# One softmax reciprocal per unit for all units, two kinds of eviction on either engine, and a new order table, in a one-core attention and feed-forward kernel

## The chip, the cores and the metric

The kernel runs on one core of a Trainium2 chip. The metric is the device time of one execution in microseconds, as the median of several runs. The kernel before takes 643.45 us (three runs, 642.06 to 644.78).

## What is computed

Attention with a position bias, then a feed-forward layer with a sigmoid gate. B = 4, H = 8, S = 576, D = 64; the feed-forward layer takes 2304 rows of 512 to 2048 and back.

```python
scores = scale * np.matmul(q, k.transpose(0, 1, 3, 2))
x = (psi_rel / psi_i)[..., None]              # log1p of |i - j| over log1p of i
h = np.maximum(x @ w1 + b1, 0.0)              # 32 hidden units per pair (i, j)
scores = scores + (h @ w2).transpose(2, 0, 1)[None]
attn = softmax(scores)                        # over the keys
x = np.matmul(attn, v)  ->  (2304, 512)
h = x @ w_in                                  # 512 x 2048
g = h * (1.0 / (1.0 + np.exp(-1.702 * h)))
out = g @ w_out                               # 2048 x 512
```

## The kernel before, in words

All of it is one program on five engines. A product of two float32 matrices is made as three products of float16 parts (high x high, high x low, low x high), so nearly every operand is split into a high part (one engine scales and rounds it) and a low part (VectorE subtracts, `lo_part`, L738).

**Bias.** For each of 5 chunks of 128 query rows (`c`, the last of 64), 8 (or 4) pieces `s` make 16 rows each: four `relu` (L619, on ScalarE L625 or VectorE L627), matrix products into PSUM (`products`, L636), an eviction from PSUM that scales each row (`bias_evict`, L646, always ScalarE), and a store to DRAM. The loads of the bias for a pair of heads come back later from there (`bias_load`, L718).

**Attention.** 72 units, each one batch entry, one chunk of rows and two heads. A unit is: `scores` (L946, TensorE), `reduce` for each head (L962, VectorE: adds the bias and finds the row maximum), `expo` for each head (L972, ScalarE: exponential and row sum), `inverse` (L979, VectorE: adds 1e-9 and scales, L982, then the reciprocal, L984, of the row sums in the tile `sm`), the split of the normalised rows (`exp_hi`, L989, on ScalarE L996 or VectorE L992, then `exp_lo`), a transpose by DMA (`turn`), and for two units together the product with v (`av`, L1049) and the split of its result into the tile `xT` (`x_pair`, L1086). The first 8 units are transposed on TensorE instead (`turn_pe`, `turn_out`, `turn_tail`). For units below `ONE_INV` = 16, `inverse` runs once, on both heads' sums (128x2), after both exponentials; from unit 16 on it runs twice, on 128x1, each after its own head's exponential.

**Feed-forward.** Ten blocks of rows (256, blocks 4 and 9 of 128). For each block 16 slices `f` of the hidden layer: `m1` (L1257, the first product, L1269), `tanh` (L1275, ScalarE), `gate_mul` (L1280, VectorE, L1283: it also frees the PSUM tile `hp`, of which there are two), `gate_hi` (L1287, ScalarE or VectorE), `gate_lo` (L1295, L1298: a subtraction on VectorE or GpSimd), `m2` (L1302, the second product, L1307). At the end of a block the result is evicted (`out_evict`, L1312, always ScalarE) and stored. `m1` of a block needs the whole of its `xT`, so the first matmul of block 0 waits for unit 7 and that of block 1 for unit 15.

**The weights** come as 64-bit numbers and are put together by three VectorE operations each (`merge`) and split (`w_split`).

**What sets the order.** All of this is put down as tasks with an engine, a cost and dependences (`Plan.add`, L34). `Plan.order` (L58) runs the tasks through a model of the engines and picks, whenever an engine is free, the ready task of the lowest priority number. The priorities are the 2,300 or so numbers of `TURNS` (L231), in the order in which tasks were added. `WHERE` (L220) says for the tasks that may run on either of two engines which one takes each (`either`, L553). What comes out is one fixed sequence of instructions per engine, each engine working through its own in that sequence and waiting at each instruction for what that one needs.

## Time and profile before

| what | value |
|---|---|
| runs | 642.06, 643.45, 644.78 us |
| the profiled execution's own time | 642.35 us |
| its span in the profile | 640.5 us |
| TensorE busy | 598.4 us, 93% of the span |
| VectorE busy | 516.2 us, 81% |
| ScalarE busy | 385.1 us, 60% |
| GpSimd busy | 82.2 us, 13% |
| DMA, mean rate over the span | 178 GB/s |
| first feed-forward matmul (L1269) | 114.2 us after the start |

The span is one execution on the chip. PE is TensorE, PEld its weight loads, DVE is VectorE, ACT is ScalarE, POOL is GpSimd, SP is the engine that issues most DMAs. 1.85 us of the profiled execution's own time lie outside the span. A row's "idle before, releaser" says how long the engine stood still just before the instruction and what ended that.

### The profile page before, as it was taken

The numbers are of one execution on the slowest core, as the hardware profiler recorded it, in microseconds if no ns is written. First come the engines' busy times: TensorE is split into PE (matmuls) and PEld (weight loads), VectorE is DVE, ScalarE is ACT, GpSimd is POOL, SyncE is SP. The second block draws the span as 40 slices with busy tenths as digits, with TensorE's granted clock in tenths as the row PEclk, the third lists the DMA queues.
The fourth block names the chain that finished last, engine by engine and source line by source line (L and its number), as shares of the span: only waits on it lengthen the run. The fifth ranks groups of instructions, "written<-read, shape, count | busy, mean of one in ns | idle before, by whom it ended". The sixth has DMA issues, their size and how long they took to land.

```text
span 640.5 us, 22783 instructions
## 1 busy us (share of the span) xinstructions
PE 598.4 (93%) x9648; PEld 423.2 (66%) x9648; DVE 516.2 (81%) x1381; ACT 385.1 (60%) x851; POOL 82.2 (13%) x123
## 2 busy tenths in 40 slices
PE   5769778899999999999999989999999999999997
PEld 2225556666756676668676677768667777787775
DVE  7999988999999957885978999887987978823333
ACT  7987785789798638653745764554554656322122
POOL 3000000113211012201020111100112100111021
PEclk9769989999999999999999999999999999999999
DMA  9996966699999795999999999997996995620000
GB/s 267 306 309 175 302 188 177 109 255 243 255 254 195 140 230 145 195 197 206 212 176 257 204 229 158 202 176 136 172 223 143 174 154 105 114 44 31 2 35 18
DMA packets 239030, 113.96 MB, mean 178 GB/s; under 512 B 218576, under 2 KB 223312, under 8 KB 238928
## 3 DMA queue, kind: packets, MB, share of 16 engines
q1 hardware_dynamic: 236240, 107.83, 78.2%
q10 hardware_dynamic: 2688, 4.68, 2.1%
q8 instruction: 75, 1.23, 0.8%
q14 instruction: 27, 0.22, 0.1%
HBM read 52.85 MB, written 15.34 MB: 106 GB/s over the span
## 4 chain that ended last, share of the span: by engine, by line
PE 70%; DVE 17%; ACT 6%; DMA 4%; issue 2%; ACTq 0%; SPq 0%; DVEq 0%
PE op L1307 25%; PE hp L1269 24%; PE hp L1062 7%; PE sp L957 7%; DVE wide L966 3%; DVE wide L739 3%; PE sp L644 3%; ACT wide L625 2%; DMA wide<-scr 2%; PE op L644 2%; PE op L1016 1%; DVE th L1283 1%; DVE v L739 1%; DVE narrow L1199 1%; DVE narrow L1203 1%
## 5 line engine op out<-in xcount | busy, mean ns | idle before, releaser
L1269 PE MATMUL hp<-xT,w 128*64 128x256 f16 (+1 forms) x3840 | 207.3, 262 | 7.6 <-DVE th L1283 4.3
L1269 PEld LDWEIGHTS <-w 128*64 128x64 f16 x3840 | 189.7, 110 | 26.7 <-issue 16.9
L1307 PE MATMUL op<-w,gT 128*64 128x512 f16 x1728 | 203.5, 380 | 0.0
L1298 POOL TENSOR_TENSOR gT<-th,gT 128x256 f16<-128x256 f32 (+1 forms) x102 | 77.1, 757 | 551.0 <-ACT gT L1291 278.5
L1307 PEld LDWEIGHTS <-gT 128*64 128x64 f16 x1728 | 96.9, 110 | 73.9 <-issue 6.3
L975 ACT ACTIVATE wide<-wide,sm 128x576 f32<-128x576 f32 x144 | 110.7, 769 | 50.0 <-DVE sm L966 47.4
L1277 ACT ACTIVATE th<-hp 128x256 f32<-128x256 f32 (+1 forms) x160 | 57.1, 357 | 115.7 <-PE hp L1269 94.1
L1283 DVE SCALAR_TENSOR_TENSOR th<-th,hp 128x256 f32<-128x256 f32 (+1 forms) x160 | 62.1, 390 | 64.4 <-ACT th L1277 63.6
L966 DVE CUSTOM_DVE_ANT_0 wide<-sp,wide 128x576 f32<-128x576 f32 x144 | 105.7, 750 | 6.1 <-PE sp L957 4.2
L739 DVE SCALAR_TENSOR_TENSOR wide<-wide,sm,wide 128x576 f16<-128x576 f32 x128 | 106.2, 843 | 3.0 <-ACT wide L996 2.7
L957 PE MATMUL sp<-wide,narrow 64*128 64x512 f16 (+2 forms) x720 | 67.3, 326 | 6.0 <-DVE sm L966 4.0
L625 ACT ACTIVATE wide<-tab,bp 128x576 f32<-128x576 f32 x86 | 62.8, 774 | 0.0
L1062 PEld LDWEIGHTS <-v 128*64 128x64 f16 x2160 | 58.4, 111 | 5.7 <-issue 2.7
L1062 PE MATMUL hp<-wide,v 128*64 128x128 f16 (+1 forms) x2160 | 60.0, 214 | 1.7 <-DVE th L1283 1.7
L957 PEld LDWEIGHTS <-narrow 64*128 64x128 f16 (+1 forms) x960 | 28.4, 98 | 41.2 <-issue 23.5
L996 ACT ACTIVATE wide<-wide,sm 128x576 f16<-128x576 f32 x65 | 48.8, 768 | 7.8 <-DVE sm L984 5.3
L1291 ACT CAST gT<-th 128x256 f16<-128x256 f32 (+1 forms) x76 | 29.1, 383 | 27.2 <-PE op L1307 13.6
L644 PE MATMUL op<-wide,pk 128*32 128x512 f32 (+1 forms) x224 | 25.0, 522 | 11.2 <-ACT narrow L647 6.0
L992 DVE TENSOR_SCALAR wide<-wide,sm 128x576 f16<-128x576 f32 x63 | 34.5, 556 | 0.2
L1298 DVE TENSOR_TENSOR gT<-th,gT 128x256 f16<-128x256 f32 (+1 forms) x58 | 23.1, 397 | 8.7 <-ACT gT L1291 7.6
L982 DVE TENSOR_SCALAR sm<-sm 128x1 f32<-128x1 f32 (+1 forms) x128 | 19.8, 154 | 12.7 <-ACT wide L975 12.3
L627 DVE TENSOR_SCALAR wide<-tab,bp 128x576 f32<-128x576 f32 x58 | 29.1, 530 | 0.8 <-PE sp L644 0.8
(74 smaller groups left out, 496.4 us busy)
## 6 DMA issues: line engine op xcount, KB each, us to landing
wide<-scr SPq DMA_DIRECT2D x32, 576.0 KB, 5.1
scr<-narrow SPq DMA_DIRECT2D x31, 288.0 KB, 3.0
wide<-in_moe_w_out_dram SPq DMA_DIRECT2D x16, 512.0 KB, 5.8
wide<-in_moe_w_in_dram SPq DMA_DIRECT2D x16, 512.0 KB, 5.2
wide<-in_k_dram SPq DMA_DIRECT2D x16, 256.0 KB, 5.1
narrow<-in_q_dram SPq DMA_DIRECT2D x16, 256.0 KB, 4.3
out_dram<-narrow ACTq DMA_DIRECT2D x16, 256.0 KB, 3.9
wide<-scr SPq DMA_DIRECT2D x8, 288.0 KB, 4.6
```

The costliest lines, as they stand in the source:

```text
L625: nc.scalar.activation(out=h, in_=tv, func=ACTF.Relu, bias=bp[:, pb:pb + 1])
L644: nc.tensor.matmul(to[32 * r:32 * r + 32], lhsT=w2b, rhs=rhs, start=True, stop=True)
L739: nc.vector.scalar_tensor_tensor(out=out, in0=in0, scalar=scale, in1=in1, op0=ALU.mult, op1=ALU.subtract)
L957: nc.tensor.matmul(pair[64 * e:64 * e + m, a, cs], lhsT=qt[r, x, hp + e, q0:q0 + m], rhs=k_of(b, hp + e, y, cs)[r], start=i == 0, stop=i == 2,
L966: nc.vector.tensor_tensor_reduce(out=slot(("a32", u))[:, cs], in0=slot(("sp", u)).rearrange("p (h a) n -> p h (a n)", h=2)[:, a, 0:S], in1 ...
L975: nc.scalar.activation(out=t, in_=t, func=ACTF.Exp, scale=-1.0, bias=sm[:, a:a + 1], accum_out=sm[:, 2 + a:3 + a])
L1062: nc.tensor.matmul(o[64 * a:64 * a + 64, po], lhsT=vt[:, x, vc:vc + 64], rhs=t[:, 9 * y + k0, po], start=kb < 0 and i == 0, stop=kb == 3 a ...
L1269: nc.tensor.matmul(p[y0:y0 + FF, :n], lhsT=wi16[:, f // 4, cc, z, w0:w0 + FF], rhs=r, start=i == 0, stop=i == 11, skip_group_check=FF < 128,)
L1277: nc.scalar.activation(out=slot(("th", j, f))[:, :n], in_=slot(("hp", j, f))[:, :n], func=ACTF.Tanh, scale=0.851 / (XS * WIS))
L1283: nc.vector.scalar_tensor_tensor(out=th, in0=th, scalar=1.0, in1=slot(("hp", j, f))[:, :n], op0=ALU.add, op1=ALU.mult)
L1298: (nc.vector if on("low", NF * j + f) == "V" else nc.gpsimd).tensor_tensor(out=gt[:, 1, :n], in0=th, in1=gt[:, 0, :n], op=ALU.subtract)
L1307: nc.tensor.matmul(o[y0:y0 + FF, i], lhsT=gt[:, z, 128 * i + y0:128 * i + y0 + FF], rhs=wo16[:, NF - 1 - f, y, :], start=f == 0 and n3 == ...
```

## The change

Three things change in the code, and the two tables with them. `ONE_INV` goes from 16 to 72, so `inverse` runs once for both heads in all units. `bias_evict` and `out_evict` may run on either engine, by two new strings in `WHERE`. All the other strings of `WHERE` and the whole of `TURNS` are replaced. The diff also adds branches that no unit takes here (`POOL_EXP`, `RELU_POOL` and `WARM` are empty).

```diff
     WHERE = {
-        'khi': 'AAAAAAVV',
+        'evict': 'AAAAAAAAAAAAAAAAAAAAAAAAAAAVAAAAVAAV',
+        'out': 'AAAAAAAAVAAAAVVAVAVA',
+        'khi': 'AAAAAAAA',
...
     TURNS = [
-        -105731, 7219, -6608, 12047, -1336, 20364, -21356, -1727, 7198, -17301, -23943, -24621, -26077, -10464,
...
+        -5778, -1874, -6302, -696, -6131, 3502, 428, 4509, -1771, 3505, -12098, -21823, -18034, -12144, -8006, -4740,
...
-    ONE_INV, TAB_LATE = 16, False
+    ONE_INV, TAB_LATE = 72, False
...
+    EVICT = {"A": act(S, True, 1), "V": dve(S, ptr=1)}
...
     def bias_evict(c, s):
-        nc.scalar.activation(
-            out=slot(("os", c, s))[:, 0:S], in_=bias_out(c, s)[:, 0:S], func=ACTF.Copy,
-            scale=ips[:, 8 * c + s:8 * c + s + 1],
-        )
+        t, o, x = slot(("os", c, s))[:, 0:S], bias_out(c, s)[:, 0:S], ips[:, 8 * c + s:8 * c + s + 1]
+        if on("evict", 8 * c + s) == "A":
+            nc.scalar.activation(out=t, in_=o, func=ACTF.Copy, scale=x)
+        else:
+            nc.vector.tensor_scalar(out=t, in0=o, scalar1=x, scalar2=None, op0=ALU.mult)
...
-            ev = add("ACT", act(S, True, 1), lambda c=c, s=s: bias_evict(c, s), [b],
+            ev = either("evict", 8 * c + s, lambda c=c, s=s: bias_evict(c, s), EVICT, [b],
...
     def out_evict(j, i):
-        nc.scalar.activation(out=slot(("ob", j, i))[:, 0:DM], in_=slot(("op", j))[:, i], func=ACTF.Copy,
-                             scale=1.0 / (2.0 * XS * WIS * WOS))
+        t, o, x = slot(("ob", j, i))[:, 0:DM], slot(("op", j))[:, i], 1.0 / (2.0 * XS * WIS * WOS)
+        if on("out", 2 * j + i) == "A":
+            nc.scalar.activation(out=t, in_=o, func=ACTF.Copy, scale=x)
+        else:
+            nc.vector.tensor_scalar(out=t, in0=o, scalar1=x, scalar2=None, op0=ALU.mult)
...
-            ev = add("ACT", act(512, True), lambda j=j, i=i: out_evict(j, i), [pm2],
+            ev = either("out", 2 * j + i, lambda j=j, i=i: out_evict(j, i), {"A": act(512, True), "V": dve(512)}, [pm2],
```

What the new tables do to the number of instructions on an engine (in the whole program):

| kind (line before) | VectorE before | now | the others |
|---|---|---|---|
| `inverse` on 128x1 (L982 and L984 together) | 224 | 0 | |
| `inverse` on 128x2 (both) | 32 | 144 | |
| `relu` (L627) | 58 | 51 | ScalarE +7 |
| `exp_hi` (L992) | 63 | 59 | ScalarE +4 |
| `x_pair`, high part (L1095) | 12 | 9 | ScalarE +3 |
| `k_split`, high part (L832) | 2 | 0 | ScalarE +2 |
| `gate_lo`, 256 columns (L1298) | 46 | 59 | GpSimd -13 |
| `gate_lo`, 128 columns (L1298) | 12 | 16 | GpSimd -4 |
| `bias_evict` and `out_evict` | 0 and 0 | 3 and 5 | ScalarE -3 and -5 |

TensorE has the same matmuls as before, and SP the same 278 DMAs. The order on TensorE stays nearly as it was up to the first feed-forward matmul; after that, neighbours change places.

The first place where instructions stand differently is VectorE in unit 31, one of the units from 16 on. `wide` is the unit's tile of exponentials, `sm` its row sums, `th`, `hp` and `gT` are tiles of the feed-forward layer. Before:

```order
L966 ISA wide_91,sm_78<-sp,wide_90 128x576
L966 ISA sm_78 128x1
...
L982 TENSOR_SCALAR sm_78<-sm_78 128x1
L984 RECIPROCAL sm_78<-sm_78 128x1
...
L1283 SCALAR_TENSOR_TENSOR th_121<-th_121,hp_124 128x256
L1293 CAST gT_118<-th_121 128x256
L1298 TENSOR_TENSOR gT_118<-th_121,gT_118 128x256
L739 SCALAR_TENSOR_TENSOR wide_90<-wide_91,sm_78,wide_90 128x576 x2
```

Before and now the pair of L966 rows stands there twice, once for each head; the pair L982 and L984 stood there twice before. Now:

```order
L953 ISA wide_85,sm_78<-sp,wide_99 128x576
L953 ISA sm_78 128x1
...
L1286 SCALAR_TENSOR_TENSOR th_120<-th_120,hp_123 128x256
L1296 CAST gT_118<-th_120 128x256
L969 TENSOR_SCALAR sm_78<-sm_78 128x2
L1301 TENSOR_TENSOR gT_118<-th_120,gT_118 128x256
L971 RECIPROCAL sm_78<-sm_78 128x2
L1286 SCALAR_TENSOR_TENSOR th_121<-th_121,hp_124 128x256
L1301 TENSOR_TENSOR gT_119<-th_121,gT_119 128x256
L637 TENSOR_SCALAR narrow_106<-sp,ips 128x576
L726 SCALAR_TENSOR_TENSOR wide_93<-wide_85,sm_78,wide_93 128x576 x2
```

The two pairs of small operations that followed each other became one, a product and a cast of the feed-forward layer stand ahead of it, and an eviction of a bias product (L637) stands between it and the low parts.

The second place is VectorE just ahead of the operation that completes `xT` of block 1 (the last row of each piece). Before:

```order
L1203 SCALAR_TENSOR_TENSOR narrow_105<-wide_85,narrow_105 128x512
L1283 SCALAR_TENSOR_TENSOR th_121<-th_121,hp_124 128x256
L739 SCALAR_TENSOR_TENSOR narrow_109<-narrow_108,narrow_109 128x512
L739 SCALAR_TENSOR_TENSOR w_63<-narrow_105,w_63 128x512
L966 ISA wide_98,sm_71<-sp,wide_99 128x576
L966 ISA sm_71 128x1
L739 SCALAR_TENSOR_TENSOR xT_115<-hp_123,xT_115 128x2x128
```

Now:

```order
L1206 SCALAR_TENSOR_TENSOR narrow_104<-wide_89,narrow_104 128x512
L1286 SCALAR_TENSOR_TENSOR th_120<-th_120,hp_124 128x256
L1301 TENSOR_TENSOR gT_119<-th_121,gT_119 128x256
L726 SCALAR_TENSOR_TENSOR w_63<-narrow_104,w_63 128x512
L953 ISA wide_93,sm_71<-sp,wide_98 128x576
L953 ISA sm_71 128x1
L726 SCALAR_TENSOR_TENSOR xT_115<-hp_123,xT_115 128x2x128
```

The end of block 1's `xT` stands behind the same `reduce` (unit 16, first head) as before. Over the whole stretch from the start to this row, VectorE now has one `relu`, one high part of a weight split, three 128-column copies, one cast and one `gate_lo` more, and one `exp_hi` less; the weight tiles come in another sequence.

## Rows read from the trace of the kernel before

**Rows 1.** The page's head and its part 1, busy time of each engine

```profile
span 640.5 us, 22783 instructions
PE 598.4 (93%) x9648; PEld 423.2 (66%) x9648; DVE 516.2 (81%) x1381; ACT 385.1 (60%) x851; POOL 82.2 (13%) x123
```

**Rows 2.** Busy time of each engine in five stretches

```profile
core 0: us, PE busy (x) PEld busy (x) DVE busy (x) ACT busy (x) POOL busy (x), PEclk, DMA share, GB/s
0.00:114.00 114.00, 84.85 (x804) 50.11 (x805) 101.50 (x238) 88.82 (x168) 5.02 (x21) 0.90 0.82 246
114.00:200.00 86.00, 82.42 (x1282) 57.44 (x1283) 84.11 (x199) 73.07 (x150) 17.24 (x18) 1.00 0.98 222
200.00:300.00 100.00, 100.00 (x1630) 69.57 (x1626) 78.54 (x215) 60.69 (x134) 13.66 (x17) 1.00 0.86 182
300.00:417.00 117.00, 111.80 (x2142) 82.56 (x2140) 103.84 (x310) 67.01 (x167) 17.84 (x26) 1.00 1.09 207
417.00:600.00 183.00, 183.00 (x3134) 135.52 (x3130) 134.12 (x379) 85.21 (x202) 22.55 (x30) 1.00 0.69 129
```

**Rows 3.** Timeline at 114 us and from 174 us, where TensorE starts blocks 0 and 1

```profile
114.23 1.03 PE L1269 MATMUL hp<-xT,w 128*64 128x256 f16 x15 [1.31 <-DVE xT L739]
...
174.08 1.29 PE L1269 MATMUL hp<-xT,w 128*64 128x256 f16 x20
...
176.20 0.42 DVE L739 SCALAR_TENSOR_TENSOR xT<-hp,xT 128x256 f16<-128x256 f32 x1
...
176.67 0.41 PE L1269 MATMUL hp<-xT,w 128*64 128x256 f16 x4 [1.31 <-DVE xT L739]
```

**Rows 4.** What VectorE waited for, 0 to 114 us (total, times, longest), the first

```profile
DVE bp L581 <- DMA pk<-in_pack_dram: 2.8, 1, 2.8
```

**Rows 5.** What TensorE waited for, 200 to 460 us (total, times, longest)

```profile
PE hp L1269 <- DVE th L1283: 3.6, 4, 1.6
PE hp L1062 <- DVE th L1283: 0.7, 2, 0.4
PE hp L1269 <- DVE xT L739: 0.6, 1, 0.6
```

**Rows 6.** What VectorE waited for, 200 to 460 us

```profile
DVE sm L982 <- ACT wide L975: 6.1, 15, 0.8
```

**Rows 7.** Groups of VectorE by line and form: xcount, busy us, mean ns

```profile
L992 DVE TENSOR_SCALAR wide<-wide,sm 128x576 f16<-128x576 f32 x63 | 34.5, 556 | 0.2
L627 DVE TENSOR_SCALAR wide<-tab,bp 128x576 f32<-128x576 f32 x58 | 29.1, 530 | 0.8 <-PE sp L644 0.8
...
L1298 DVE TENSOR_TENSOR gT<-th,gT 128x256 f16<-128x256 f32 x46 | 19.6, 425 | 6.3 <-ACT gT L1291 5.6
...
L984 DVE RECIPROCAL sm<-sm 128x1 f32<-128x1 f32 x112 | 17.7, 159 | 1.3
L982 DVE TENSOR_SCALAR sm<-sm 128x1 f32<-128x1 f32 x112 | 16.6, 149 | 10.6 <-ACT wide L975 10.3
...
L1095 DVE TENSOR_SCALAR xT<-hp 128x256 f16<-128x256 f32 x12 | 5.0, 419 | 1.6 <-PE hp L1062 1.6
...
L1023 DVE COPY wide<-op 128x512 f32<-128x512 f32 x2 | 1.4, 692 | 1.6 <-PE op L1016 1.6
```

**Rows 8.** Timeline of VectorE, 363.7 to 364.2 us, and two rows at 345 us

```profile
345.08 0.15 DVE L982 TENSOR_SCALAR sm<-sm 128x1 f32<-128x1 f32 x1 [0.33 <-ACT wide L975]
...
345.27 0.16 DVE L984 RECIPROCAL sm<-sm 128x1 f32<-128x1 f32 x1
...
363.73 0.17 DVE L984 RECIPROCAL sm<-sm 128x1 f32<-128x1 f32 x1
363.80 0.14 DVE L982 TENSOR_SCALAR sm<-sm 128x1 f32<-128x1 f32 x1
...
364.05 0.17 DVE L984 RECIPROCAL sm<-sm 128x1 f32<-128x1 f32 x1
364.12 0.28 DVE L1283 SCALAR_TENSOR_TENSOR th<-th,hp 128x128 f32<-128x128 f32 x1
```

## The prediction

> **What bounds the kernel now.** I read the busy shares first: TensorE is busy for 598.4 of 640.5 us, VectorE for 516.2 [rows 1]. The change leaves TensorE's work as it is, so what can be won or lost is time in which TensorE stands still. Then I cut the span into stretches [rows 2]. TensorE is idle for 29.2 us of the first 114, for 3.6 us from 114 to 200, for nothing from 200 to 300, for 5.2 us from 300 to 417, and for nothing from 417 to 600. VectorE is busy for 101.5 of 114 us at first (89%), 84.1 of 86 (98%), 79%, 89%, 73%. So there are two regimes. Up to about 177 us VectorE sets the pace: TensorE's first feed-forward matmul, at 114.23 us, and the rest of the first matmuls of block 1, at 176.67 us, both follow the VectorE operation that completes `xT`, and TensorE had stood still for 1.31 us each time [rows 3]. After that TensorE sets the pace, and loses time only where VectorE is late with a single result: every TensorE wait listed from 200 to 460 us is for VectorE, 4.9 us in seven waits, mostly for `gate_mul`, which frees `hp` [rows 5]. VectorE is late there because it works through its list in order, and because it stands at an `inverse` whose exponential isn't done (6.1 us in 15 waits [rows 6]).

> **The sum is made** against the profiled execution's own time, 642.35 us, of which 640.5 are the span; the median, 643.45, is 1.1 above it, and I carry the difference over to the median.

> **Up to the end of block 1's `xT`.** Units below 16 had one reciprocal already, so this stretch is spared none. VectorE instead gets, by the order, more to do ahead of that row. The record of a VectorE instruction overlaps the next by some 0.08 us (one of 0.15 us is followed by another's start 0.07 us later [rows 8]), so I price each at its mean less 0.08 [rows 7]: one `relu` 0.45, one high part of a weight split at most as long as an `exp_hi`, 0.48, three copies of 128 columns at 0.2 each (an estimate, half of what 256 columns take at L1095), one cast and one `gate_lo` at 0.345 each, less one `exp_hi` of 0.48: 0.45 + 0.48 + 0.6 + 0.69 - 0.48 = +1.7 us. VectorE is the bound there and TensorE has no gap from 417 to 600 us in which to catch up, so this goes to the end in full. The bounds: VectorE also stood idle for 114 - 101.5 = 12.5 us of the first 114 [rows 2], of which 2.8 are the first load [rows 4]; the other 9.7 are waits for other engines that the new table can shorten or lengthen. I leave them as they are, for the rows of the order up to the first feed-forward matmul are nearly the same; their ends, -9.7 and +9.7, go to the rivals.

> **After block 1.** VectorE loses 112 small instructions. Two rows give the price's ends: by mean time, 149 and 159 ns [rows 7], 56 pairs take 17.2 us; by the distance to the next start, 0.07 us each where that one is independent [rows 8], 7.8 us. Where the second of a pair directly follows the first the distance is 0.19 us [rows 8], and the order shows such neighbours often. I take 0.12 us each, 13.4 us. Eight `relu` less (51 for 58, with one more ahead): 3.6 us. Three `exp_hi` less 1.4, three `x_pair` 1.0, two high parts of k 1.6 (1,024 columns; an estimate from the `relu`'s 576, 0.45 x 1024/576 each). Against that twelve `gate_lo` of 256 columns and four of 128 come from GpSimd: 12 x 0.345 + 4 x 0.2 = 5.0 us; and eight evictions from ScalarE, at the 0.69 less 0.08 of the only VectorE copy of 512 columns out of PSUM [rows 7] and a little more for 576: 5.1 us. Sum: -13.4 - 3.6 - 1.4 - 1.0 - 1.6 + 5.0 + 5.1 = -10.9 us of VectorE. ScalarE takes most of what VectorE drops and is free for 40% of that time and more from 200 us on [rows 2], so I cost its part at nothing; were it not free, the price would be what it takes over less what it gives away, by VectorE's prices 3.6 + 1.4 + 1.0 + 1.6 - 5.1 = 2.5 us. GpSimd only gains time.

> **What that is worth.** VectorE is not the bound after block 1, so 10.9 us of it are not 10.9 us of the end. They can bring back at most what TensorE loses there, 5.2 us, and at least nothing, if the waits depend on places in the list and not on the load. The relief is twice the loss, and all of the waits are for VectorE [rows 5]; one wait at `inverse` falls away per unit, though the one that is left waits for the later exponential. I take four fifths: -4.2 us. What is late next is TensorE itself.

> [...]

> **Sum:** +1.7 - 4.2 = -2.5 us: 639.85 for the profiled execution, 640.9 for the median.

> **The rivals.**

> *It gains at the front as well.* The new table could let VectorE and ScalarE wait less for each other before 114 us. For it: 9.7 us of such waits are there. Against it: both orders do the same things there in almost the same sequence, with more on VectorE. With a third of them gone (3.2) and all of the later 5.2: 643.45 + 1.7 - 3.2 - 5.2 = 636.8.

> *TensorE hides more lost time than its idle time shows.* From 200 to 300 us it is busy for 100.00 us, but its weight loads for 69.57; from 417 to 600 us the loads fill 135.52 of 183, 74.1% [rows 2]. Were the whole difference lost time, 100 - 69.57/0.741 = 6.1 us could come back from there, which with the forecast makes 634.8. Against it: the first of the two stretches has bias products and other work with fewer loads per microsecond. [...] No row here tells the two readings apart.

> *Nothing comes back.* The waits come from single places in VectorE's list: `gate_mul` is behind a low part of 0.8 us or an `inverse`, wherever these are put, and VectorE was idle for 21% of the time from 200 to 300 us anyway [rows 2]. Then only the +1.7 stays: 645.2 at most, and 643.5 if the small rows at the front are hidden.

> *The front gets longer, and the kernel slower.* Place: VectorE's list ahead of the last `xT` of blocks 0 and 1, where an order that has a load, an exponential or an eviction come just behind the instruction that needs it holds up all that is queued there. Price: the 9.7 us of waits are there already; if they double, 643.45 + 9.7 + 1.7 - 4.2 = 650.7. It decides from where the delay eats the later gain and 0.5% of the time (3.2 us) besides: 3.2 + 4.2 - 1.7 = 5.7 us, that is from a first feed-forward matmul at about 120 us. For it: nearly every neighbour on VectorE changed places. Against it: on TensorE the order up to there did not.

> That the change does not do what it says is out: the order has all reciprocals on 128x2.

> **How the numbers follow.** About 0.5% of the time, 3.2 us, is what a measurement of this kernel can tell from no change: faster is below 640.2, slower above 646.7. The forecast gets 0.40 (638.5 to 643), the gain at the front too 0.22, the hidden time 0.06, nothing comes back 0.20, the longer front 0.12. Faster: 0.22 + 0.06 and 0.17 of the forecast's 0.40, 0.45. Same: the other 0.23 and 0.20, 0.43. Slower: 0.12. The range goes from 634.5 to 646.5: it leaves out the longer front and the lower part of the two gains (some 0.06).

> **What would show it.** The first feed-forward matmul within 3 us of 114.23 us, and block 1's first matmuls complete 1 to 2 us later than at 176.67; VectorE's busy time lower by some 9 us (1.7 less 10.9), ScalarE's a little higher; TensorE's idle time from 300 to 417 us at 1 to 2 us where it was 5.2, with fewer waits for `gate_mul`; the waits of `inverse` for exponentials halved in number and not longer in total. I am wrong if TensorE starts block 0 after 120 us; if TensorE's later waits are as long as before although VectorE has less to do; or if TensorE's total time from 200 us to the last matmul falls by more than 5.2 us, which would be time that its busy rows hide.

## The result, and the profile after

The changed kernel is **slower**: 650.66 us median of four runs (646.94 to 652.53) against 644.04 (642.06 to 644.78), a ratio of 1.0104 with a 95% interval of 1.0073 to 1.0134. The forecast was 640.9 us, and the range ended at 646.5. Page head and part 1 of the changed kernel's profiled execution (649.26 us):

```profile
span 647.4 us, 22644 instructions
PE 600.5 (93%) x9648; PEld 425.0 (66%) x9648; DVE 514.3 (79%) x1279; ACT 388.6 (60%) x858; POOL 66.6 (10%) x106
```

VectorE issues 102 instructions fewer than in [rows 1] and is busy for 1.9 us less, not 9. Busy times in the stretches of [rows 2]:

```profile
core 0: us, PE busy (x) PEld busy (x) DVE busy (x) ACT busy (x) POOL busy (x), PEclk, DMA share, GB/s
0.00:114.00 114.00, 84.51 (x804) 50.33 (x805) 101.14 (x240) 86.81 (x162) 5.10 (x21) 0.91 0.81 241
114.00:200.00 86.00, 81.03 (x1266) 56.52 (x1267) 83.97 (x193) 70.58 (x145) 13.35 (x15) 1.00 0.92 219
200.00:300.00 100.00, 99.71 (x1614) 68.59 (x1612) 79.06 (x192) 66.84 (x141) 11.15 (x14) 1.00 0.91 184
300.00:417.00 117.00, 110.94 (x2083) 79.98 (x2081) 98.15 (x260) 70.08 (x177) 14.39 (x21) 1.00 1.06 205
417.00:600.00 183.00, 182.34 (x3175) 137.02 (x3172) 137.65 (x351) 83.14 (x201) 15.99 (x23) 1.00 0.71 133
```

From 300 to 417 us VectorE is busy for 5.7 us less, and TensorE is idle for 6.1 us where it was 5.2. The waits did not shrink, they moved. What TensorE waited for from 200 to 460 us (total, times, longest), to be set against [rows 5]:

```profile
PE sp L944 <- DMA narrow<-narrow: 2.1, 2, 1.7
PE op L1310 <- issue: 1.5, 1, 1.5
PE sp L944 <- DVE sm L953: 1.3, 2, 0.9
PE hp L1272 <- DVE th L1286: 0.4, 2, 0.2
PE op L1310 <- POOL gT L1301: 0.4, 2, 0.2
PE op L1310 <- ACT narrow L1318: 0.4, 1, 0.4
PE hp L1061 <- DVE th L1286: 0.2, 1, 0.2
```

The waits of first matmuls for `gate_mul` (3.6 us before) are 0.4 us. In their place stand waits that the kernel before did not have: scores wait for a transfer and for the `reduce` that frees `sp`, second matmuls for a low part on GpSimd and for an eviction. The 1.5 us that the list puts down to "issue" are no new wait: the kernel before has that stall too, listed there under `gate_mul` (more of it below).

To place the loss I took, for every PE step of the four kinds that repeat, the time from its first matmul to the next step's, less an estimate of the least that such a step takes (1.31 us a first matmul of 256 rows, 1.29 a second, 1.68 a pair of attention outputs, 0.74 scores; halves for half the rows), and summed what is over. Times are counted so that the first feed-forward matmul is at 114 us; the least times are rough (in the trace of the kernel before the shortest such steps take 1.31, 1.29, 1.67 and 0.84 us), so only differences between kernels mean something. The sums are larger than TensorE's idle time, since it counts as busy in part of what is lost: from 417 to 600 us the changed kernel has 0.7 us more of idle time, and from 420 to 600 us 1.7 us more are lost.

| us lost by TensorE | 114-200 | 200-340 | 340-420 | 420-600 | from 600 | sum |
|---|---|---|---|---|---|---|
| before | 7.3 | 2.9 | 9.2 | 2.1 | 0.3 | 21.9 |
| changed | 8.0 | 2.9 | 11.1 | 3.8 | 1.7 | 27.5 |
| changed, second trace | 8.0 | 2.9 | 12.8 | 4.0 | 1.7 | 29.4 |

The 5.6 us of difference to the first trace and 0.9 us of a later first feed-forward matmul (115.08 us for 114.23) make 6.5 of the 6.9 us of span; the rest is the last eviction and its store. The two largest single places are at 381 and at 622 to 626 us.

### The profile page after: what moved, and what is told of

It reads as the page before. It is cut to its first block, busy times and chain, and to the rows that moved or that the text cites. A ratio compares the mean times of both kernels' runs of the same rounds, so it can differ in the third digit from the quotient of the medians.

```text
span 647.4 us, 22644 instructions
## 1 busy us (share of the span) xinstructions
PE 600.5 (93%) x9648; PEld 425.0 (66%) x9648; DVE 514.3 (79%) x1279; ACT 388.6 (60%) x858; POOL 66.6 (10%) x106
## 5 line engine op out<-in xcount | busy, mean ns | idle before, releaser
L1310 PEld LDWEIGHTS <-gT 128*64 128x64 f16 x1728 | 98.5, 110 | 73.7 <-issue 7.3
L1301 POOL TENSOR_TENSOR gT<-th,gT 128x256 f16<-128x256 f32 (+1 forms) x85 | 61.5, 725 | 569.4 <-ACT gT L1294 334.3
L726 DVE SCALAR_TENSOR_TENSOR wide<-wide,sm,wide 128x576 f16<-128x576 f32 x128 | 104.6, 841 | 5.1 <-ACT wide L991 4.6
L611 ACT ACTIVATE wide<-tab,bp 128x576 f32<-128x576 f32 x93 | 66.7, 770 | 0.1
L991 ACT ACTIVATE wide<-wide,sm 128x576 f16<-128x576 f32 x69 | 51.2, 766 | 8.7 <-DVE sm L971 4.7
L1301 DVE TENSOR_TENSOR gT<-th,gT 128x256 f16<-128x256 f32 (+1 forms) x75 | 29.8, 399 | 12.5 <-ACT gT L1294 10.3
L630 PE MATMUL op<-wide,pk 128*32 128x512 f32 (+1 forms) x224 | 24.3, 513 | 12.5 <-ACT narrow L635 5.5
L989 DVE TENSOR_SCALAR wide<-wide,sm 128x576 f16<-128x576 f32 x59 | 31.5, 553 | 0.1
L1296 DVE CAST gT<-th 128x256 f16<-128x256 f32 (+1 forms) x81 | 22.3, 278 | 10.4 <-PE op L1310 8.0
L630 PE MATMUL sp<-wide,pk 128*32 128x512 f32 (+1 forms) x352 | 26.5, 443 | 2.0 <-DVE sm L953 1.9
```

The lines of the kernel that those rows point to most:

```text
L611: nc.scalar.activation(out=h, in_=tv, func=ACTF.Relu, bias=bp[:, pb:pb + 1])
L726: nc.vector.scalar_tensor_tensor(out=out, in0=in0, scalar=scale, in1=in1, op0=ALU.mult, op1=ALU.subtract)
L991: nc.scalar.activation(out=o, in_=t, func=ACTF.Identity, scale=r)
L1301: (nc.vector if on("low", NF * j + f) == "V" else nc.gpsimd).tensor_tensor(out=gt[:, 1, :n], in0=th, in1=gt[:, 0, :n], op=ALU.subtract)
L1310: nc.tensor.matmul(o[y0:y0 + FF, i], lhsT=gt[:, z, 128 * i + y0:128 * i + y0 + FF], rhs=wo16[:, NF - 1 - f, y, :], start=f == 0 and n3 == ...
```

## The experiments

The ratios are to the kernel before, run beside each of them, with 95% intervals. "In place" means: the program is planned with one kernel's table, costs and choices, so that the order is that kernel's, and the choices or the instructions are exchanged only when the steps are written out. Each engine then has its steps where that order puts them.

**Again.** No edit.

> The changed kernel once more, nothing edited. All theories: 1.010 of the kernel before, within 0.003 (649 to 652 us against 644). It shows whether the stalls of TensorE read in the first trace of it stand at the same places in a second one: 1.5 us at 347 us (both kernels have it at the same matmul), 1.7 us at 379 us, 0.3 us at 580 us, 0.8 us at 624 to 626 us. If the two traces differ by more than 2 us in the total of these, part of the loss is chance of the single execution.

1.0107 [1.0074, 1.0141], 649.62 us. The second trace has the stalls at the same places, and but for one they are of about the same size: the one at 347 us takes 2.4 us instead of 1.5, which makes up part of the 1.7 us between the two rows of the table from 340 to 420 us. Its first feed-forward matmul comes at 113.6 us instead of 115.1. So the places of the later waits belong to the kernel; 1.5 us at the front and 1.7 us from 340 to 420 us are chance of the single execution.

**The reciprocal alone.** Two kernels in the order of the kernel before.

```
 def inverse(u, a, part):
+    if u >= ONE_INV and a == 0 and u not in APART:
+        return
-    r = small[u % 8][:, 2:4] if u < ONE_INV else small[u % 8][:, 2 + a:3 + a]
+    r = small[u % 8][:, 2 + a:3 + a] if u in APART else small[u % 8][:, 2:4]
```

In `merge_in_place` no unit is apart, and `exp_hi(u, 0)` and `exp_lo(u, 0)` are held back until the pair is written where they stood ahead of it. In unit 27 the pair stands ahead of the first head's exponential there, so that head is scaled by another value; the instructions are the same. In `merge_where_free` 14 units are apart and nothing is held back.

> Only the reciprocal is changed, in the order and with the engines of the kernel before: in units from 16 on one pair of VectorE instructions works on both heads, at the place of the second head's pair; the 13 high parts (and 3 low parts) of the first head that stood ahead of that place come right behind it. Theory A (the order costs, the reciprocal gains): 641 to 643.5 us against 644. Theory B (waiting for the second exponential holds up VectorE): 646 us or more. Theory C (the reciprocals' time is hidden, as VectorE is not the bound after 177 us): 643.5 to 644.5.

1.0049 [1.0030, 1.0067], 646.56 us, as theory B had it.

> merge_in_place once more, but the 13 units in which the first head's high part stood ahead of the second head's pair (16, 17, 18, 24, 28, 32, 37 to 40, 45, 50, 64) and unit 27 keep two pairs, so nothing is put off; 42 units are merged, 84 VectorE instructions fewer. Theory O (the merging costs by what it puts off behind the later exponential): 642.7 to 644 us against 643.5, no slower than the kernel before. Theory P (fewer places to wait at make the waits longer, whatever is put off): 645 us or more, and VectorE's waits for exponentials from 200 to 420 us above 6 us.

1.0007 [0.9986, 1.0028], 643.16 us. What VectorE waited for from 200 to 460 us, in the first and in the second (the row of `inverse`, [rows 6]):

```profile
DVE sm L990 <- ACT wide L981: 9.7, 14, 1.2
```

```profile
DVE sm L990 <- ACT wide L981: 7.3, 14, 1.0
```

Before it was 6.1 us in 15 waits. With fewer instructions VectorE comes earlier to the pair and waits there longer, in both; yet only the kernel that also puts 13 high parts off is slower. So theory O holds on the time: merging costs where a high part stood between the two pairs and is put off behind the later exponential, and is free, and worth nothing, where nothing is put off. (The two kernels differ by unit 27 as well; in the trace of `merge_in_place` its pair starts at 259 us, and TensorE loses no more than before from 250 to 270 us.) Theory P was right that the waits grow and wrong that this costs. In the trace of `merge_in_place` TensorE falls back by 1.3 us from 177 to 192 us, where units 16 to 18, the first with a high part put off, are worked on.

**VectorE's relief alone.** The first of the two instructions is left out, each head keeps its own reciprocal, nothing is moved: in units from 16 on (`reciprocal_alone`), or in all (`reciprocal_alone_all`, below).

```
-    AS = 1024.0
+    AS = 1.0
...
-    if part == 0:
-        nc.vector.tensor_scalar(out=r, in0=r, scalar1=1.0e-9, scalar2=1.0 / AS, op0=ALU.add, op1=ALU.mult)
-    else:
+    if part:
         nc.vector.reciprocal(out=r, in_=r)
```

> The kernel before, order and engines unchanged, in which units from 16 on do without the first of the pair (add 1e-9, divide by 1024): VectorE issues 112 instructions less, as many as in the change, but each head keeps its own reciprocal and waits for its own exponential alone. The factor 1024 is taken out of x_pair's scale instead, and the 1e-9 is left out. Theory I (the relief is worth something, and the merged pair's wait for the later exponential ate it): 639 to 642 us against 643.2, VectorE busy for 6 to 7 us less, and waits of VectorE for exponentials from 200 to 420 us at about 5.3 us as before (8.3 in merge_in_place). Theory C (VectorE's relief is hidden): 642.7 to 643.7 us. Theory J (any edit shifts the later waits by 1 to 3 us for the worse, the order being fitted to the old times): 644 us or more.

0.9990 [0.9970, 1.0009], 643.54 us.

> reciprocal_alone, and the first instruction of the pair falls away in the 16 units below 16 as well (the factor 1024 is set to 1 everywhere; the 1e-9 is left out). These 16 instructions stand where VectorE is busy for 89 to 98 percent and sets the pace. Theory Q (a VectorE instruction is worth its distance to the next, 0.07 to 0.19 us, up to 177 us and nothing after): 1.1 to 3.0 us earlier than reciprocal_alone at block 1's first matmuls and at the end, 640.5 to 642.4 us against 643.5. Theory C for the whole kernel (hidden everywhere): 643 to 644.

1.0003 [0.9980, 1.0026], 642.97 us. Part 1 of the page of the first, and its stretch from 300 to 417 us:

```profile
PE 598.0 (93%) x9648; PEld 423.2 (66%) x9648; DVE 507.3 (79%) x1269; ACT 384.5 (60%) x851; POOL 83.2 (13%) x123
```

```profile
300.00:417.00 117.00, 110.97 (x2136) 82.30 (x2134) 100.92 (x272) 67.09 (x168) 18.54 (x26) 1.00 1.08 205
```

VectorE is busy for 8.9 us less than in [rows 1], 2.9 of them in the stretch where TensorE lost most [rows 2], and TensorE is idle there for 6.0 us as against 5.2. Theory C holds: the relief is hidden. VectorE stands still instead: its waits listed from 200 to 460 us sum to 43.1 us for 36.7. The two largest rows, before and then in `reciprocal_alone`:

```profile
DVE th L1283 <- ACT th L1277: 19.5, 18, 4.4
DVE sm L982 <- ACT wide L975: 6.1, 15, 0.8
```

```profile
DVE th L1306 <- ACT th L1300: 22.4, 22, 4.4
DVE sm L990 <- ACT wide L981: 5.6, 13, 0.7
```

`gate_mul` waits longer for its `tanh`; the wait at `inverse` does not grow when nothing is merged. The relief is hidden ahead of 177 us as well, or is too small to be seen: theory Q's 1.1 to 3.0 us are excluded for the larger part by an interval that ends at 0.9980 (1.3 us).

**The choices of engine.** In place, in the order of the kernel before:

```
 plan.order()
+WHERE.update(NOW)    # NOW: of the changed kernel's strings those named
```

> The kernel before, and of the change only that eight evictions (three of bias products, five of outputs) are VectorE's, at the places that they have in its order. Theory E (an eviction pair split over two engines runs one after the other, as the second waits for the first, and VectorE's queue holds up what is behind it): 645 us or more against 643.5, with 0.2 to 1.5 us lost at the end of each of blocks 4, 6, 7 and 8. Theory F (the evictions fall into VectorE's free time): 643 to 644 us.

1.0023 [1.0004, 1.0041], 645.04 us.

> The kernel before, and of the change only the engine of the 160 low parts of the gate: 42 go from GpSimd to VectorE and 25 the other way, at their places. Theory D (single choices of engine that don't fit the order cost): 645 to 648 us, with new waits of TensorE for VectorE at 200 to 320 us. Theory K (their number alone counts, 17 more of 0.35 us on an engine that isn't the bound): 643 to 644.

1.0023 [1.0008, 1.0038], 645.26 us. Each of these two parts costs some 1.5 us, by intervals that only just leave out 1; E and D, which had 645 us or more, are nearer than F and K.

> The kernel before in its order, with the changed kernel's engines for relu, high parts of the exponentials, of the gate, of x, of the weights and of k, and the copies of the turned attention; evictions and low parts of the gate as before, two reciprocals. If the parts' costs add up, it is what is left of new_choices_old_order's 8.5 us less 3.2 (merging), 1.5 (evictions) and 1.5 (low parts): 645.5 to 646.5 us against 643.5. If the parts cost by standing together, it is 643.5 to 644.5; if these are the choices that cost, 647 or more.

1.0130 [1.0095, 1.0164], 650.84 us.

> As merge_in_place, and every choice of engine is that of the changed kernel (evictions, relu, high and low parts), each at the place that its step has in the order of the kernel before. Theory A (the order costs): at most 646 us. Theory D (the choices of engine cost, above all evictions split over two engines and low parts on VectorE): 648 us or more, about as slow as the changed kernel.

1.0133 [1.0110, 1.0155], 651.05 us. (Unit 27 as in `merge_in_place`.) The strings differ far more than their sums: of 160 low parts 42 go to VectorE and 25 come back; 71 high parts of the gate, 40 of the exponentials, 25 `relu` and 15 high parts of x change sides; with the smaller strings it is 236 steps. All but the low parts and the evictions cost 8 us by themselves in an order that was not made for them, as much as everything together, so the parts do not add up. Theory D holds for that order, A falls. The largest single step in the trace of `other_choices_old_order` is at 206 us, where the attention outputs wait 2.3 us for the `gate_mul` that frees `hp`; in the kernel before they do not wait.

> The order of the changed kernel with the choices of engine of the kernel before, and again two reciprocals per unit from 16 on (both at the place of the single one). Theory A (the order costs): 650 us or more, as the order is the same and 112 small VectorE instructions come on top. Theory D (the choices cost): 643 to 646 us. An order that was made for the new choices may also suffer from the old ones, so a time far above 652 says little of D, one near 644 says much.

1.0202 [1.0184, 1.0220], 656.23 us, 6 us above the changed kernel. The reverse mismatch costs even more, so this run speaks for neither: order and choices are fitted to each other. The change as a whole (1.0104 and 1.0107) is clearly better than the new order with the old choices; against the new choices in the old order (1.0133) the intervals overlap, so how much of their cost the new order gives back is not shown.

**The evictions in the new order.** In place, `evict` and `out` all on ScalarE.

> The changed kernel with all evictions on ScalarE again, in its own order otherwise. Theory E: 647.5 to 649 us against 650, with the stall of TensorE at 622 to 626 us (1.4 us) down to 0.5 or less and outputs' second eviction 0.5 us behind the first instead of 0.7. Theory F: 650 us, no change.

1.0128 [1.0095, 1.0161], 651.61 us: no gain. Theory E falls as far as time goes, although what it says of the pair can be read. From the timeline of the changed kernel at the end of block 8:

```profile
622.13 1.53 PE L1272 MATMUL hp<-xT,w 128*64 128x128 f16 x48
622.36 0.69 DVE L1320 TENSOR_SCALAR narrow<-op 128x512 f32<-128x512 f32 x1 [2.03 <-PE op L1310]
...
623.09 0.60 ACT L1318 ACTIVATE narrow<-op 128x512 f32<-128x512 f32 x1 [2.59 <-DVE narrow L1320]
...
623.73 0.84 PE L1310 MATMUL op<-w,gT 128*64 128x512 f16 x6
...
624.15 0.28 ACT L1280 ACTIVATE th<-hp 128x128 f32<-128x128 f32 x1 [0.47 <-ACT narrow L1318]
...
624.46 0.29 DVE L1286 SCALAR_TENSOR_TENSOR th<-th,hp 128x128 f32<-128x128 f32 x1 [0.95 <-ACT th L1280]
...
624.80 0.86 PE L1272 MATMUL hp<-xT,w 128*64 128x128 f16 x24 [0.23 <-DVE th L1286]
...
626.19 0.86 PE L1272 MATMUL hp<-xT,w 128*64 128x128 f16 x24 [0.53 <-DVE th L1286]
```

ScalarE's eviction waits for VectorE's, though they read different halves of `op`; `tanh` stands behind it, `gate_mul` behind `tanh`, and TensorE has one second matmul (x6) to cover that. But the split pair is not what makes the stall. In `evict_scalar` one engine evicts both halves, and the next two first matmuls wait 0.23 and 0.84 us for `gate_mul`, against 0.23 and 0.53 above:

```profile
625.59 1.09 ACT L1322 ACTIVATE narrow<-op 128x512 f32<-128x512 f32 x2 [1.86 <-PE op L1314]
...
627.80 0.86 PE L1276 MATMUL hp<-xT,w 128*64 128x128 f16 x24 [0.23 <-DVE th L1290]
...
629.50 0.86 PE L1276 MATMUL hp<-xT,w 128*64 128x128 f16 x24 [0.84 <-DVE th L1290]
```

What remains is that one second matmul stands there. The kernel before goes on at this place with three:

```profile
617.23 1.09 ACT L1313 ACTIVATE narrow<-op 128x512 f32<-128x512 f32 x2 [0.80 <-PE op L1307]
...
618.37 2.13 PE L1307 MATMUL op<-w,gT 128*64 128x512 f16 x18
```

**Steps put back.** Three places of the new order, each with a wait that its traces have and that of the kernel before has not. The tail: one number of the table, so that block 9's sixth first matmul comes behind three second matmuls. q: SP's load of a bias goes behind the transposing transfer. v: VectorE's low parts go behind two sums.

```
-    ... 65547, 66643, 60175, 58922, ...
+    ... 65547, 66643, 63000, 58922, ...
 def bias_load(u, c, hp, now=False):
+    if u == 46 and not now:
+        late.append(lambda: bias_load(u, c, hp, True))
+        return
 def turn_q(b, c):
     ...
+    if (b, c) == (2, 1):
+        late.pop()()
```

(v in the same way: `split_v(3, 0, 1)` is kept for the end of `reduce(41, 1)`.)

> The changed kernel with two of its steps moved: block 9's sixth first matmul comes behind the third second matmul of that block (it stands behind the first), and SP's load of the bias for unit 46 comes behind the transposing transfer of q for batch 2, chunk 1, instead of ahead of it. Theory L (the new order loses its time at single places, and what is lost there is lost at the end): TensorE's stall at 622 to 626 us goes from 1.4 to 0.3 us or less, the one before unit 44's scores at 381 us from 1.7 to 0.7 or less: 647 to 648.3 us against 650. Theory M (from 320 to 410 us VectorE sets the pace, and what TensorE gains at 381 us is lost again before 410): only the tail's 1.1 us come back, 648.5 to 649.2, and the stalls from 382 to 415 us grow by what the one at 381 lost.

Tail and q: 1.0051 [1.0030, 1.0073], 646.92 us, some 3.4 us less than the changed kernel.

> The changed kernel with block 9's sixth first matmul behind the third second matmul of that block, nothing else. Theory L (every single wait counts): 648.6 to 649.2 us against 650 and 643.3, the wait at 622 to 626 us down from 1.4 to 0.4 us. Theory M (only waits outside of 320 to 410 us count, and this one gave the whole of two_fixes' gain): 647 to 648.3.

1.0103 [1.0067, 1.0139], 651.55 us.

> The changed kernel with SP's load of the bias for unit 46 behind the transposing transfer of q (batch 2, chunk 1), nothing else. Theory L: 648 to 648.8 us, the wait before unit 44's scores at 381 us down from 1.7 to 0.3 us or less. Theory M (time won there is lost before 410 us): 649.5 to 650.5, the wait gone and others up to 415 us longer.

1.0076 [1.0049, 1.0103], 648.89 us. In the trace of `tail_fix` TensorE loses 0.8 us from 600 us on, where it was 1.7; the time shows none of it, but its interval is 2.3 us to either side. For the transfer of q the medians differ by 1.8 us (1.0104 less 1.0076), as L has it, but the intervals overlap. In its trace the waits for that transfer are down to 0.3 us (2.1 in the changed kernel), and by the measure of the table 1.5 us are won from 370 to 380 us and 0.9 lost again from 380 to 390, as M has it. So neither move is shown to gain by itself. Together they do: the three kernels that have both are at 1.0051, 1.0051 and 1.0057, the changed kernel at 1.0104 and 1.0107. From the timeline of the changed kernel, SP's queue and the scores that wait:

```profile
373.56 0.56 SPq L710 DMA_DIRECT2D wide<-scr  x1
374.23 1.44 SPq L757 DMA_TRANSPOSE narrow<-narrow  x1
375.78 9.01 SPq L1046 DMA_TRANSPOSE wide<-wide  x2
...
381.46 0.39 PE L944 MATMUL sp<-wide,narrow 64*128 64x512 f16 x2 [1.74 <-DMA narrow<-narrow]
```

and of `two_fixes`, where the scores do not wait:

```profile
372.30 1.57 SPq L762 DMA_TRANSPOSE narrow<-narrow  x1
373.97 1.10 SPq L715 DMA_DIRECT2D wide<-scr  x1
...
378.88 0.39 PE L951 MATMUL sp<-wide,narrow 64*128 64x512 f16 x2
```

> two_fixes, and VectorE's four low parts of v for batch 3 (2.6 us), which stand between the two instructions of unit 40's reciprocal and ahead of the sums of unit 41 (the reduce of both heads), come behind these sums. Theory L (single places, each worth what TensorE waits there): the wait before unit 42's scores goes from 1.5 to 0.3 us or less, and the kernel takes 645 to 646 us against 647 for two_fixes and 643.3 for the kernel before. Theory M (what is won between 320 and 410 us is lost again before 410): 646.5 to 647.5, the wait gone and others up to 415 us longer by as much.

1.0051 [1.0029, 1.0073], 647.13 us: nothing gained, though the wait is gone. Timeline of `two_fixes`, where the scores of unit 42 wait for sums that stand behind the low parts of v:

```profile
362.41 2.64 DVE L731 SCALAR_TENSOR_TENSOR v<-wide,v 64x128 f16<-64x128 f32 x4
...
365.06 0.73 DVE L960 CUSTOM_DVE_ANT_0 wide<-sp,wide 128x576 f32<-128x576 f32 x1
...
366.53 0.39 PE L951 MATMUL sp<-wide,narrow 64*128 64x512 f16 x2 [1.51 <-DVE sm L960]
```

In `three_fixes` these scores start at 364.27 us without a wait, but from there to 372 us TensorE loses 1.2 us more than in `two_fixes`. Here M is nearer.

**TensorE's own stall.** Matmuls of one column of zeros at the start, 40 or 96 of them in the kernel before, 88 in `three_fixes`:

```
 def inverse_pe():
     p = slot("pc")
+    for _ in range(96):
+        nc.tensor.matmul(p[0:64, 0:1], lhsT=zero, rhs=zero[:, 0:1], start=True, stop=True)
```

> The kernel before with 96 matmuls of one column of zeros more on TensorE at its start, whose result is overwritten; it computes the same. Theory G (TensorE stands still 1.5 us at 347 us because its next 256 instructions, fetched by DMA, come late: the 256 before them are 120 short matmuls with their weight loads and last 2.5 us only; 192 instructions more at the start shift the cuts so that no such piece is left): 641.5 to 642.5 us against 643.5, without that stall. Theory H (the stall is a wait for VectorE's gate_mul, as the profile puts it down): 643.5 us or, as the start gets 2 us longer, up to 645.5, and the stall stays.

1.0015 [0.9995, 1.0036], 644.45 us.

> The same with 40 such matmuls, which by theory G shifts the cuts to the worst places: of the pieces of 256 instructions some at 327, 340 and 553 us then hold 120 short matmuls and last 2.3 to 3.2 us. Theory G: 646 to 648 us, slower than before, with stalls of TensorE of 1 to 2.5 us behind 328, 341 and 553 us that no semaphore ends. Theory H: within 1 us of before_plus96.

1.0017 [0.9992, 1.0042], 643.92 us.

> three_fixes with 88 matmuls of one column of zeros more at TensorE's start, which shifts the cuts between its pieces of 256 instructions so that none falls together with 120 short matmuls at 344 us. By theory G the stall of 1.7 us at 347 us, and that of 0.3 us at 580, are gone from the trace. Theory L: 643.5 to 644.8 us, 1.2 to 1.7 less than three_fixes. Theory M: within 0.5 us of three_fixes, as before_plus96 was of the kernel before, with other waits up to 415 us longer.

1.0057 [1.0035, 1.0080], 646.95 us. G is right about the places, but for one, and wrong about the time. With 96, and with 88 in `three_fixes`, the stall at 347 us is gone. With 40 two stalls that no semaphore ends stand at 335 and 350 us, of 0.7 and 1.2 us (none at 553). With 96, TensorE comes to 347 us a microsecond early and loses 1.9 us more than the kernel before at four steps from 348 to 378 us. What is won there is lost again at once, as M says.

No version beat the kernel before; the best are those whose interval holds 1 (`reciprocal_alone`, `reciprocal_alone_all`, `merge_where_free`, and the two with dummy matmuls, `before_plus96` and `before_plus40`).

## Why the prediction was wrong, step by step

- **What bounds the kernel.** TensorE's work stayed, as said, and the loss is time in which it stands still. But one of the waits that I read as VectorE's is none: of the 3.6 us for `gate_mul` in [rows 5] the longest, 1.6, is the stall at 347 us. In the kernel before this matmul starts 0.42 us behind the end of the `gate_mul` that is named; in `before_plus96`, in the same order, it starts 0.83 us ahead of that `gate_mul`, so it does not wait for it. The kernel before, and then `before_plus96`:

```profile
346.50 0.42 DVE L1283 SCALAR_TENSOR_TENSOR th<-th,hp 128x256 f32<-128x256 f32 x1
...
347.34 0.92 PE L1269 MATMUL hp<-xT,w 128*64 128x256 f16 x13 [1.57 <-DVE th L1283]
```

```profile
346.31 1.39 PE L1296 MATMUL hp<-xT,w 128*64 128x256 f16 x22
...
347.14 0.41 DVE L1310 SCALAR_TENSOR_TENSOR th<-th,hp 128x256 f32<-128x256 f32 x1
```

- **Up to block 1's `xT`, +1.7 us.** The first trace has +0.9 at block 0 and +1.1 at block 1 (177.81 us for 176.67). But seven traces of kernels in the new order that differ only later put the first feed-forward matmul at 113.6 to 116.5 us, 114.9 in the mean, and six in the old order at 113.2 to 115.4, 114.4 in the mean. So up to block 0 some 0.5 us of the term are seen, within what chance does to a single trace.
- **VectorE's relief, -10.9 us.** Mis-sized in its first row. I priced the 112 instructions at 0.12 us each, 13.4; `merge_in_place` has as many fewer and VectorE is busy for 516.2 - 509.6 = 6.6 us less, 0.059 each, and `reciprocal_alone`, with 112 fewer too, for 8.9 us less, 0.079 each. I should have taken the distance between starts of independent neighbours, 0.07 us [rows 8], that I had beside it. The sum also left out the casts of `gate_hi` (four more of 256 columns on VectorE and seven fewer of 128), which is small. For the whole change the busy time fell by 1.9 us.
- **What that is worth, four fifths of 5.2 us, -4.2.** This is the step that failed, and a right size of the relief would not have saved it. `reciprocal_alone` takes 8.9 us off VectorE, leaves all else, and the kernel takes 0.999 [0.997, 1.0009] of the time: a gain of 1.9 us at most, where four fifths of 5.2 were forecast. With less to do VectorE only waits longer for the next `tanh` (22.4 us for 19.5), so TensorE's waits hang on the place of single instructions in VectorE's list and not on its load. My rival "nothing comes back" had this mechanism and got 0.20. With this step at nothing the sum gives 645.2 us, which is still inside the range. What took the result out of the range is the bound that I put beside the step, "at least nothing": I let the new order win back TensorE's waits or leave them, and gave it no price for making new ones. It made 5.0 us more of lost time from 200 us on (the table: 11.1 for 9.2, 3.8 for 2.1, 1.7 for 0.3).
- **"The one that is left waits for the later exponential."** I named it and gave it no price. By itself, in the old order, it costs 3.2 us (1.0049), through the 13 high parts put off. What it costs in the new order, no run tells.
- **ScalarE's part at nothing.** I counted net numbers (eight `relu`, three `exp_hi`) and priced VectorE's share. Gross, 236 steps change engines, and in the old order the 161 of them in `other_choices_old_order` cost 8 us by themselves. Whether that is ScalarE's load or the place of the steps, no run tells apart; nor how much of it is left in the new order.
- **The rivals.** "The front gets longer" gave 650.7 us, near the result, but by luck, for it was wrong about the place: the first feed-forward matmul is at 115 us, not 120. The rival I lacked is the same mechanism later: an order in which a transfer, a sum or a matmul comes one step too late for the engine that waits. Two such places together are worth some 3.4 of the 6.6 us, by three kernels that have both moves and two measurements of the changed kernel; the share of each is not shown. Of TensorE's hidden time nothing was seen: it got no shorter from 200 us to the last matmul.
- **What stays open.** The other 3.2 us. `two_fixes` still loses 25.1 us by the measure of the table, 3.2 more than the kernel before, some 2 of these in steps that lose less than 0.3 us each; no single place was found for them. Why the time won at 347 and 366 us came back as other waits, was not settled either.

What I had given as a sign of error is what came: TensorE's later waits as long as before, although VectorE has less to do.

## What to carry to other kernels

Before pricing the relief of an engine that is not the bound, take the instructions away and leave everything else: one such run tells whether there is anything to win (here 8.9 us less of VectorE's time, and 0.9990 of the kernel's). Give a new order a price below zero as well: this one made waits that were not there, 2.1 us for one transfer. The order tables here are fitted to the choices of engine that they were made with (with most or all of the other's choices they take 1.0130 and 1.0202 of the time of the kernel before); judge a change of it by the gross number of steps that change place or engine, and look in the new trace for single waits that the old one does not have, on the transfer queue too. Merging two small instructions was free here where nothing stood between them (1.0007), and cost time where it made the first input's users wait for the second (1.0049).

## What the runs showed of the hardware

In 17 of the 20 traces TensorE stands still for 0.9 to 2.6 us with all its semaphores given, each time at the same place in its list, the 4,561st or 4,562nd matmul. In the changed kernel:

```profile
347.35 0.40 PE L1310 MATMUL op<-w,gT 128*64 128x512 f16 x1
349.28 0.79 PEld L1310 LDWEIGHTS <-gT 128*64 128x64 f16 x10 [1.82 <-issue]
349.28 1.05 PE L1310 MATMUL op<-w,gT 128*64 128x512 f16 x8 [1.53 <-issue]
```

```profile
q8 instruction: 75, 1.23, 0.8%
```

The engine's two rows make 19,296 instructions, 75 times 256 and some, and in the traces the pieces start 255 instructions apart on average. In the changed kernel the piece before the stall began at 346.8 us and took 1.0. The 256 instructions ahead of the stall hold 115 short matmuls of attention outputs and last 3.2 us (3.8 in the kernel before): counted off from there in lots of 256 from 114 us on, it is the shortest lot in either kernel, where the median is 7.8 us.

That the stall moves with the number of instructions ahead of it is shown by three kernels. With 40 matmuls more it is again the 4,561st that comes late, now one in the middle of an attention output, and the other stall stands exactly 256 matmuls, or 512 instructions, earlier. That late pieces are the cause is a reading, but a close one: in the 17 traces TensorE goes on 1.3 to 1.7 us behind the end of such a piece's transfer, whether it had stood still for 0.9 us or for 2.6.

Two evictions from the two halves of one PSUM tile on two engines ran one after the other, the second waiting on the first's semaphore and starting 0.03 us behind its end, in all three such pairs of the changed kernel (at 519, 582 and 622 us). The pair at 622 us frees the tile 0.24 us later than two on ScalarE do in the kernel before (1.36 us behind the last matmul for 1.12). Whether the two could overlap without that semaphore, no run tells.
